# A fixed order for the opening of an attention-plus-expert-layer kernel: engine queues in the order of the text, block means by small transfers, weights staged in whole chunks

## The chip, the cores and the metric

The kernel runs on one core of a Trainium2 chip. The core has five engines that work side by side: TensorE (matrix products, PE in the profile), VectorE (DVE), ScalarE (ACT), GpSimd (POOL) and SyncE (SP), which here only issues transfers. Each engine takes its instructions strictly in the order of its own queue and waits on semaphores for the others; transfers run on sixteen DMA engines. The metric is the time of one execution on the device in microseconds. A change in the median of under 0.5% is not told from none here.

## What is computed

The reference is local attention with block summaries, followed by a two-layer expert with a rational activation. Batch 4, 8 heads, 768 positions, head size 64; the 3072 tokens of width 512 then go through 512 to 2048 to 512.

```python
k_sum = k.reshape(B, H, nb, 32, D).max(axis=3)
v_sum = v.reshape(B, H, nb, 32, D).mean(axis=3)
scores_l = where(|pos_q - pos_k| < 16, scale * q @ k.T, -1e9)
scores_s = scale * q @ k_sum.T + log(32)
a = softmax(concat([scores_l, scores_s]))      # with 1e-9 added to the sum
x = a @ concat([v, v_sum])                     # then heads side by side: 3072 x 512
h = x @ w_in
P = a0 + a1*h + a2*h^2 + a3*h^3
Q = 1 + |b0|*|h| + |b1|*h^2
out = (P / (Q + 1e-6)) @ w_out
```

The weights arrive as 64-bit floats and are turned into 32-bit values on the chip.

## The kernel before

**Tiles.** Attention works on 48 pieces ("halves") of 64 query positions. One half has four pairs of heads; each query sees 96 keys of its window and 24 block maxima (120 columns). Three functions carry a half: `att_a` (scores on TensorE into `sc`, mask and minimum on VectorE, exponentials on ScalarE, the reciprocal on VectorE, the scaling by it on GpSimd: tile `ss`), `att_b` (four transposes into `pt` on TensorE, a copy to `pts` on ScalarE) and `att_c` (products with values into `av`, stored as a rounded high part `xh` and a remainder `xl`). Eight halves make a group of 512 tokens.

**The expert.** There are six groups (g = 0 to 5) and 16 chunks of the hidden width (fc = 0 to 15), so 96 steps. A step multiplies into `h` (`moe1`, twelve matmuls: high by high, low weights by high, high by low), evaluates the activation (`gelu`: six ScalarE operations with a logarithm and an exponential, five or six on VectorE, and one on GpSimd that makes the low part `gl`), and three steps later (LAG) multiplies the result of the earlier chunk into four accumulators `po` (`moe2`). Halves of the next group's attention are spread over the steps.

**Weights.** A chunk is loaded as 64-bit words (1 MB for both matrices) into a staging tile `wr`, and `w_split` converts it: ScalarE rescales the upper words (L295), VectorE shifts the lower words (L298) and joins them in (L299), ScalarE rounds to the high part (L302), GpSimd makes the low part (L304). Chunks 0 to 7 end in `wearly`, the others in `w` tiles. Before, chunks 0 to 7 are staged whole in four buffers `wl`. Chunks 8 to 15 are staged as two halves of 512 KB in the pool `stage`, which has two buffers and also holds rows for the key maxima `kr` and value sums `vr`. Converted weights stay in SBUF for all groups.

**The opening.** The first eight halves are computed before step 0. Their block means of values come from TensorE (`vf`, L153, raw values times a matrix of 1/32), and are copied by ScalarE into rows 96 to 119 of six value tiles (L158 to L160); halves 6 and 7 reuse the tiles of halves 0 and 1.

**Order.** The text is traced and a scheduler with its own timeline reorders instructions of each engine between their dependencies; `tc.high_priority` shifts its priorities. In the 96 steps the matmuls are kept in the order of the text (`chained`); before step 0 no engine is. The string FIRST gives the order of the first loads on SP's queue.

Of the kernel before, what the change touches and what calls it, by code (L numbers as in the profile page):

```python
# [10 lines left out]
I32 = mybir.dt.int32  # L11
# [3 lines left out]
PSUM = bass.MemoryType.PSUM  # L15

# [25 lines left out]
CVL = 5  # L42
NEARLY = 3
SOFF = 12
VLAG = 5
NWARM = 6
FIRST = "Q0 K0 K1 V0 K2 K3 Q1 V1 S V2 W0 V3 F W1 V4 W2 G W3 V5"
AVGAT = 4
# [10 lines left out]
def tile_kernel(ctx, tc, qw_in, kraw, kwin, vpad, vred, wio, a, b, cmask, cident, cavg, out):  # L59
# [6 lines left out]
    wl = ctx.enter_context(tc.tile_pool(name="wl", bufs=NLATE))  # L66
# [7 lines left out]
    chained = []  # L74

    def mm(*args, **kw):
        ins = nc.tensor.matmul(*args, **kw)  # L77
        if chained:
            tc.keep_in_program_order(ins)
# [20 lines left out]
    def setup():  # L100
# [4 lines left out]
        nc.vector.tensor_scalar_mul(cs[:, 0:6], coef, SH)  # L105
        nc.vector.tensor_scalar_mul(cs[:, 6:7], cs[:, 5:6], -1.0)
        nc.vector.tensor_tensor(cs[:, 5:6], cs[:, 5:6], cs[:, 6:7], op=ALU.max)
        nc.vector.memset(cs[:, 7:8], C1 * SH)
# [16 lines left out]
    def key_sum(bi, pr):  # L125
        kr = sums.pop(("k", bi, pr))
        ins = nc.vector.tensor_reduce(ksum[bi][:, pr, :], kr.rearrange("p (n k) -> p n k", k=BLK), axis=AX.X, op=ALU.max)
        if bi:
            tc.keep_in_program_order(ins)
# [8 lines left out]
    def value_sum(bi, c):  # L138
        vs, vr = vsum[bi], sums.pop(("v", bi, c))
        tc.keep_in_program_order(nc.vector.tensor_reduce(vs[:, c, :], vr, axis=AX.X, op=ALU.add))  # L140
        if c == NVC - 1:
            nc.vector.tensor_scalar_mul(vs, vs, 1.0 / BLK)
# [9 lines left out]
    def value_average(bi, av, vt, i):  # L152
        nc.tensor.matmul(av[:NK, :], avg[:, AVGW - NK - 4 * i:AVGW - 4 * i], vt[i], start=(i == 0), stop=(i == len(vt) - 1))  # L153
        if i < len(vt) - 1:
            return
        if bi == 0:
            for i in range(2):
                nc.scalar.copy(vw[i][NKW:NK, :], av[NKW:NK, :])  # L158
            for t in vres[2:6]:
                nc.scalar.copy(t[NKW:NK, :], av[NKW:NK, :])  # L160
        else:
            t = gp.tile([NK, DM], F32, tag="gh", name="vn")
            nc.scalar.copy(t[NKW:NK, :], av[NKW:NK, :])
# [10 lines left out]
    def att_a(jj, pool=None, tag="a", sbuf=None):  # L174
        bi, j = divmod(jj, NJ)
        kt, qt = kw[jj % 2], qw[jj % 2] if jj >= HPG else qres[:, jj]
        if j < 2 and bi > 0 or jj in (HPG, HPG + 1):
            nc.vector.tensor_copy(kt[:, NKC - 1], ksum[bi])
        mt = mask[:, 0 if j == 0 else (2 if j == NJ - 1 else 1), :]
        sc = (pool or ps_a).tile([P, 512], F32, tag=tag, name=f"sc{jj}")  # L180
        for pr in range(NPAIR):
# [4 lines left out]
            for lo, hi, keys in parts:  # L186
                for e in range(2):
                    rows = slice(e * D, (e + 1) * D)
                    mm(sc[rows, pr * NK + lo:pr * NK + hi], qt[rows, pr, :], keys[rows], start=True, stop=True)
# [3 lines left out]
        for pr in range(NPAIR):  # L193
            nc.vector.tensor_tensor_reduce(  # L194
                out=ss[:, pr, :], in0=sc[:, pr * NK:(pr + 1) * NK], in1=mt, op0=ALU.add, op1=ALU.min,
                scale=-SCALE, scalar=3.0e38, accum_out=sm[:, 0, pr:pr + 1])
        for pr in range(NPAIR):
# [320 lines left out]
```

## Time and profile before

| what | value |
|---|---|
| median of three runs | 726.27 us (725.87 to 729.55) |
| profiled execution | 721.27 us |
| its span, first to last instruction | 719.5 us |
| busy share of the span: TensorE, VectorE, ScalarE, GpSimd | 94%, 84%, 66%, 44% |
| moved by DMA | 60.8 MB, 84 GB/s on the mean |

A line number such as L298 is a line of the kernel; where a helper records all matmuls (L77), one tells them by tile names. "out<-in" names the tile written and the tiles read, x16 a count. The span is cut into the opening, group 0 (16 steps) and the rest. Idle time of an engine counts only where the end waits for it.

### The profile page before, as it was taken

What the parts mean: (1) busy time and instruction counts of PE and PEld (TensorE: products, weight loads), DVE (VectorE), ACT (ScalarE), POOL (GpSimd) and SP (SyncE); (2) the same over time, 40 slices, a digit from 0 to 9 for tenths busy, and PEclk for the clock granted to TensorE, in tenths of its full rate; (3) what the DMA queues carried; (4) which work ended last, traced back from release to release, by engine and by line L of the source; (5) the groups of instructions that cost most, each with busy time, mean ns of one, the idle gap of its engine ahead of it and who ended that gap; (6) DMA issues with size and microseconds to landing.
All of it is one profiled execution on the core that took longest, in us unless ns stands there. A gap on an engine that the chain in (4) does not pass through costs nothing.

```text
span 719.5 us, 12003 instructions
## 1 busy us (share of the span) xinstructions
PE 677.4 (94%) x4196; PEld 526.5 (73%) x4196; DVE 604.6 (84%) x1189; ACT 471.5 (66%) x1058; POOL 313.7 (44%) x328
## 2 busy tenths in 40 slices
PE   8887879948999999999999999999999999999997
PEld 5555657736777777777777777777777777888886
DVE  4688997797988898887789998878978878998885
ACT  2896776656776666776666766656776755775562
POOL 0785645645554354444343345443453353232231
PEclk9887989978999999999999999999999999999999
DMA  9982254333124231113112332111121200010001
GB/s 288 368 279 89 85 167 139 118 98 118 40 76 149 87 91 32 44 62 119 47 43 74 103 95 69 48 45 30 51 82 45 60 12 0 1 59 1 1 1 59
DMA packets 30681, 60.76 MB, mean 84 GB/s; under 512 B 3748, under 2 KB 15396, under 8 KB 29596
## 3 DMA queue, kind: packets, MB, share of 16 engines
q1 hardware_dynamic: 29916, 59.54, 26.0%
q8 instruction: 33, 0.54, 0.3%
q10 hardware_dynamic: 576, 0.25, 0.1%
q14 instruction: 28, 0.23, 0.1%
q0 software_dynamic: 128, 0.20, 0.1%
HBM read 53.44 MB, written 6.34 MB: 83 GB/s over the span
## 4 chain that ended last, share of the span: by engine, by line
PE 70%; DVE 9%; ACT 7%; DMA 6%; POOL 4%; issue 4%; SPq 0%; DVEq 0%; POOLq 0%; ACTq 0%
PE po L77 31%; PE h L77 29%; PE sc L77 4%; DMA wr<-in_wio_dram 4%; PE av L77 3%; PE pt L221 3%; ACT ss L198 2%; POOL ss L203 2%; DVE tq L326 2%; POOL w L304 1%; DVE wr L299 1%; ACT wr L295 1%; PE vf L153 1%; DVE gh L331 1%; DMA kres<-in_kraw_dram 1%
## 5 line engine op out<-in xcount | busy, mean ns | idle before, releaser
L334 POOL TENSOR_TENSOR gl<-tu,ta 128x512 fp32r<-128x512 f32 x96 | 132.8, 1383 | 219.5 <-DVE tu L333 143.5
L203 POOL TENSOR_SCALAR ss<-ss,sm 128x120 f32<-128x120 f32 x192 | 132.5, 707 | 142.1 <-ACT ta L328 105.3
L326 DVE SCALAR_TENSOR_TENSOR tq<-tq,cs,ta 128x512 f32<-128x512 f32 x96 | 117.4, 1223 | 41.9 <-ACT ta L324 41.1
L323 ACT ACTIVATE tq<-h 128x512 f32<-128x512 f32 x96 | 57.2, 596 | 121.5 <-PE h L77 121.5
L77 PE MATMUL po<-w,gh 128*128 128x512 f32 x384 | 130.6, 422 | 0.0
L77 PE MATMUL po<-wearly,gh 128*128 128x512 f32 x384 | 130.1, 420 | 0.0
L327 ACT ACTIVATE ta<-tq,cs 128x512 f32<-128x512 f32 x96 | 69.6, 725 | 60.6 <-DVE tq L326 60.2
L77 PE MATMUL h<-xh,wearly 128*128 128x512 f32 x384 | 98.2, 399 | 1.5 <-ACT xh L251 1.1
L77 PE MATMUL h<-xh,w 128*128 128x512 f32 x384 | 95.4, 390 | 0.0
L331 DVE SCALAR_TENSOR_TENSOR gh<-tu,cs,ta 128x512 fp32r<-128x512 f32 x96 | 73.4, 765 | 22.3 <-ACT ta L328 14.4
L77 PEld LDWEIGHTS h<-xh,wearly 128*128 128x128 f32 x384 | 73.7, 193 | 17.8 <-ACT xh L251 1.3
L77 PEld LDWEIGHTS h<-xh,w 128*128 128x128 f32 x384 | 72.2, 188 | 15.9
L198 ACT ACTIVATE ss<-ss,sm 128x120 f32<-128x120 f32 x192 | 73.0, 383 | 11.0 <-DVE sm L194 10.9
L77 PEld LDWEIGHTS po<-w,gh 128*128 128x128 f32 x384 | 67.5, 195 | 16.4 <-issue 3.5
L77 PEld LDWEIGHTS po<-wearly,gh 128*128 128x128 f32 x384 | 65.5, 192 | 16.8 <-issue 3.4
L333 DVE SCALAR_TENSOR_TENSOR tu<-tu,cs,tq 128x512 f32<-128x512 f32 x96 | 75.1, 782 | 3.1
L77 PE MATMUL po<-w,gl 128*128 128x512 f32 x192 | 76.7, 400 | 0.0
L77 PE MATMUL po<-wearly,gl 128*128 128x512 f32 x192 | 75.9, 395 | 0.0
L221 PE MATMUL pt<-ident,ss 128*120 128x128 f32 x192 | 53.6, 291 | 23.6 <-POOL ss L203 23.3
L325 ACT ACTIVATE tu<-h,cs 128x512 f32<-128x512 f32 x96 | 75.0, 782 | 0.0
L330 DVE SCALAR_TENSOR_TENSOR tu<-tu,cs,h 128x512 f32<-128x512 f32 x96 | 71.6, 746 | 2.9
L332 DVE SCALAR_TENSOR_TENSOR tq<-tq,gh 128x512 f32<-128x512 f32 x96 | 67.6, 704 | 2.8
(63 smaller groups left out, 1043.3 us busy)
## 6 DMA issues: line engine op xcount, KB each, us to landing
vw<-in_vpad_dram SPq DMA_DIRECT2D x44, 192.0 KB, 2.7
wr<-in_wio_dram SPq DMA_DIRECT2D x8, 1024.0 KB, 10.9
wr<-in_wio_dram SPq DMA_DIRECT2D x16, 512.0 KB, 3.9
kw<-in_kwin_dram SPq DMA_DIRECT2D x40, 192.0 KB, 2.7
out_dram<-o SPq DMA_DIRECT2D x24, 256.0 KB, 2.1
qw<-in_qw_dram SPq DMA_DIRECT2D x40, 128.0 KB, 2.6
kr<-in_kraw_dram SPq DMA_DIRECT2D x12, 384.0 KB, 3.3
vr<-in_vred_dram SPq DMA_DIRECT2D x8, 384.0 KB, 3.5
```

The source lines that it names most:

```text
L77: ins = nc.tensor.matmul(*args, **kw)
L198: nc.scalar.activation(ss[:, pr, :], ss[:, pr, :], AF.Exp, scale=-1.0, bias=sm[:, 0, pr:pr + 1], accum_out=sm[:, 1, pr:pr + 1])
L203: nc.gpsimd.tensor_scalar(ss[:, pr, :], ss[:, pr, :], sm[:, 1, pr:pr + 1], 1.0, op0=ALU.mult, op1=ALU.mult)
L221: ins = nc.tensor.transpose(out=pt[:NK, pr * P:(pr + 1) * P], in_=ss[:, pr, :], identity=ident)
L325: nc.scalar.activation(tu, h, AF.Identity, scale=cs[:, 3:4], bias=cs[:, 2:3])
L326: nc.vector.scalar_tensor_tensor(out=tq, in0=tq, scalar=cs[:, 5:6], in1=ta, op0=ALU.mult, op1=ALU.add)
L327: nc.scalar.activation(ta, tq, AF.Ln, bias=cs[:, 7:8])
L330: nc.vector.scalar_tensor_tensor(out=tu, in0=tu, scalar=cs[:, 1:2], in1=h, op0=ALU.add, op1=ALU.mult)
L331: nc.vector.scalar_tensor_tensor(out=gh, in0=tu, scalar=cs[:, 0:1], in1=ta, op0=ALU.add, op1=ALU.mult)
L332: nc.vector.scalar_tensor_tensor(out=tq, in0=tq, scalar=C1 * SH, in1=gh, op0=ALU.add, op1=ALU.mult)
L333: nc.vector.scalar_tensor_tensor(out=tu, in0=tu, scalar=cs[:, 0:1], in1=tq, op0=ALU.add, op1=ALU.subtract)
L334: nc.gpsimd.tensor_tensor(gl, tu, ta, op=ALU.mult)
```

## The change

1. **A wrapper `Kept` around four engines.** While an engine is in `strict`, each of its instructions is tied behind the one recorded before it, so its queue has the order of the text. All four are strict from the first score product to the end of the string EARLY. Then VectorE, ScalarE and GpSimd are released, but everything they do later stays tied behind their last strict instruction. TensorE stays strict to the end.
2. **EARLY** writes the order of the opening: `s` scores and minima, `e` exponentials and scaling, `p`/`P` transposes (with `P` the copy to `pts` is on VectorE), `v` a product of the means, `w` and `x` the two parts of converting chunk 0, `c` products with values, `W` a whole conversion. Chunks 1 and 2 come after the last `c`.
3. **Means by transfers.** ScalarE copies them to two value tiles; six others get them by a transfer of 24 rows each from the first, on SP's queue. Halves 6 and 7 have value tiles of their own.
4. **Weights staged whole.** All chunks but 15 are loaded as 1 MB into four separately named buffers; the load of a later chunk is issued when an earlier one is rounded. VectorE's two operations take both matrices at once (1024 columns in place of twice 512).
5. CVL goes from 5 to 3 (a conversion is recorded three steps ahead of its use), two attention loads move ahead of the opening's computation, and the means of batch 1 move from before step 0 into steps 0 and 1.

```diff
-CVL = 5
+CVL = 3
-FIRST = "Q0 K0 K1 V0 K2 K3 Q1 V1 S V2 W0 V3 F W1 V4 W2 G W3 V5"
+FIRST = "K0 Q0 K1 K2 K3 S Q1 F W0 V0 V1 V2 V3 V4 V5 V6 V7 W1 A8 A9 W2 G W3"
+EARLY = ("s0 s1 e0 s2 e1 s3 e2 v0 s4 e3 P0 v1 s5 e4 P1 v2 s6 e5 P2 v3 s7 w0 e6 P3 v4 e7 P4 x0 v5 c0 P5 c1 P6 c2 "
+         "P7 c3 c4 c5 c6 c7 W1 W2")
...
+    class Kept:
...
+                out = getattr(self.engine, name)(*args, **kw)
+                for ins in nc.cur_bb.bb.instructions[n:]:
+                    if ins.engine == out.ins.engine:
+                        if self.last is not None:
+                            tc.add_manual_dep(ins, self.last, ORDERED, reason="order of the text")
+                        if self in strict:
+                            self.last = ins.name
...
             for i in range(2):
-                nc.scalar.copy(vw[i][NKW:NK, :], av[NKW:NK, :])
-            for t in vres[2:6]:
-                nc.scalar.copy(t[NKW:NK, :], av[NKW:NK, :])
+                act.copy(vw[i][NKW:NK, :], av[NKW:NK, :])
+            for t in vres[2:]:
+                nc.sync.dma_start(out=t[NKW:NK, :], in_=vw[0][NKW:NK, :])
...
     def w_load(fc):
+        kind = F32 if wio.dtype == F32 else I32
+        words = DM if kind == F32 else 2 * DM
+        if fc == NFC - 1:
+            raws[fc] = [(slice(s, s + 1), stage.tile([P, 1, words], kind, tag="st", name=f"wr{fc}_{s}")) for s in range(2)]
+        else:
+            k = fc % NLATE if fc < NFC - NLATE else fc - (NFC - NLATE) + 1
+            raws[fc] = [(slice(0, 2), wl.tile([P, 2, words], kind, tag=f"wl{k}", name=f"wr{fc}"))]
+        for s, raw in raws[fc]:
+            nc.sync.dma_start(out=raw, in_=wio[fc, :, s, :].bitcast(kind))
+
+    def w_join(fc):
...
+            act.activation(top, top, AF.Prelu, scale=2.0**-112, alpha=2.0**32)
+            dve.tensor_single_scalar(l32, l32, 29, op=ALU.logical_shift_right)
+            dve.scalar_tensor_tensor(out=h32, in0=h32, scalar=3, in1=l32,
+                                     op0=ALU.logical_shift_left, op1=ALU.bitwise_or)
+
+    def w_round(fc):
...
+            act.copy(wt[:, 0, s, :], w)
+            for i in range(s.start, s.stop):
+                gps.tensor_tensor(wt[:, 1, i, :], w[:, i - s.start], wt[:, 0, i, :], op=ALU.subtract)
+        ahead = fc + NLATE if fc < NFC - 2 * NLATE else fc + NLATE - 1
+        if fc != NFC - 2 * NLATE and ahead < NFC:
+            w_load(ahead)
...
+    strict |= {pe, dve, act, gps}
+    for what in EARLY.split():
...
+    strict -= {dve, act, gps}
...
-        at(max(fc - CVL, 0), lambda fc: w_split(fc, wr.pop(fc) if fc in wr else w_load(fc)), fc)
+        at(max(fc - CVL, 0), w_split, fc)
...
+        if step in (0, 1):
+            if step == 0:
+                vf = ps_o.tile([P, DM], F32, tag="o", name="vf1")
+            for i in range(3 * step, 3 * step + 3):
+                value_average(1, vf, fv1, i)
```

The next excerpts show the built order of a queue. The first number in a name is the program's own: `wr5` is the staging tile of chunk 5 (`wr8_1` its second half), `av6` belongs to half 6, `gl0_2` to group 0, chunk 2. In the changed kernel every operation through the wrapper has the line L87.

VectorE at the end of the opening, before:

```order
L298 TENSOR_SCALAR wr5_0_676<-wr5_0_676 128x512 x2
L252 TENSOR_TENSOR xl0_412<-av2_517,xh0_411 128x4x64
L299 SCALAR_TENSOR_TENSOR wr5_0_676<-wr5_0_676 128x512 x2
L252 TENSOR_TENSOR xl0_412<-av3_535,xh0_411 128x4x64
L252 TENSOR_TENSOR xl0_412<-av4_546,xh0_411 128x4x64
L298 TENSOR_SCALAR wr6_0_749<-wr6_0_749 128x512 x2
L299 SCALAR_TENSOR_TENSOR wr6_0_749<-wr6_0_749 128x512 x2
L252 TENSOR_TENSOR xl0_412<-av5_557,xh0_411 128x4x64
L252 TENSOR_TENSOR xl0_412<-av6_568,xh0_411 128x4x64
L298 TENSOR_SCALAR wr7_0_828<-wr7_0_828 128x512 x2
L299 SCALAR_TENSOR_TENSOR wr7_0_828<-wr7_0_828 128x512 x2
L252 TENSOR_TENSOR xl0_412<-av7_579,xh0_411 128x4x64
```

VectorE at the same place, after the change:

```order
L87 TENSOR_TENSOR xl0_495<-av3_550,xh0_494 128x4x64
L87 TENSOR_TENSOR xl0_495<-av4_561,xh0_494 128x4x64
L87 TENSOR_TENSOR xl0_495<-av5_572,xh0_494 128x4x64
L87 TENSOR_TENSOR xl0_495<-av6_583,xh0_494 128x4x64
L87 TENSOR_TENSOR xl0_495<-av7_594,xh0_494 128x4x64
L87 TENSOR_SCALAR wr1_158<-wr1_158 128x1024
L87 SCALAR_TENSOR_TENSOR wr1_158<-wr1_158 128x1024
L87 TENSOR_SCALAR wr2_164<-wr2_164 128x1024
L87 SCALAR_TENSOR_TENSOR wr2_164<-wr2_164 128x1024
```

The conversions of chunks 1 to 7, which stood among and before the remainders `xl`, now stand behind the last of them.

GpSimd in the first steps, before:

```order
L304 TENSOR_TENSOR wearly_103<-wr7_0_828,wearly_103 128x512 x2
L334 TENSOR_TENSOR gl0_0_645<-tu0_0_643,ta0_0_641 128x512
L203 TENSOR_SCALAR ss8_729<-ss8_729,sm8_730 128x120 x4
L334 TENSOR_TENSOR gl0_1_706<-tu0_1_704,ta0_1_702 128x512
L203 TENSOR_SCALAR ss9_801<-ss9_801,sm9_802 128x120 x4
L334 TENSOR_TENSOR gl0_2_778<-tu0_2_776,ta0_2_774 128x512
L304 TENSOR_TENSOR w8_905<-wr8_0_906,w8_905 128x512
L334 TENSOR_TENSOR gl0_3_857<-tu0_3_855,ta0_3_853 128x512
L203 TENSOR_SCALAR ss10_971<-ss10_971,sm10_972 128x120 x4
L304 TENSOR_TENSOR w8_905<-wr8_1_908,w8_905 128x512
L334 TENSOR_TENSOR gl0_4_939<-tu0_4_937,ta0_4_935 128x512
```

GpSimd at the same place, after the change:

```order
L87 TENSOR_TENSOR wearly_103<-wr6_619,wearly_103 128x512 x2
L87 TENSOR_TENSOR gl0_0_638<-tu0_0_636,ta0_0_634 128x512
L87 TENSOR_TENSOR gl0_1_683<-tu0_1_681,ta0_1_679 128x512
L87 TENSOR_SCALAR ss9_782<-ss9_782,sm9_783 128x120 x4
L87 TENSOR_TENSOR wearly_103<-wr7_657,wearly_103 128x512 x2
L87 TENSOR_TENSOR w8_1063<-wr8_732,w8_1063 128x512 x2
L87 TENSOR_TENSOR w8_1063<-wr9_815,w8_1063 128x512 x2
L87 TENSOR_TENSOR w10_1219<-wr10_890,w10_1219 128x512 x2
L87 TENSOR_TENSOR gl0_2_759<-tu0_2_757,ta0_2_755 128x512
L87 TENSOR_TENSOR w10_1219<-wr11_981,w10_1219 128x512 x2
L87 TENSOR_SCALAR ss10_943<-ss10_943,sm10_944 128x120 x4
L87 TENSOR_TENSOR gl0_3_836<-tu0_3_834,ta0_3_832 128x512
```

Before, one half chunk stands between two activations' low parts; now the low part of chunk 2 stands behind four whole chunks of weights.

SP's queue where the means are copied (a row `x2` is two transfers), after the change only, since there were no such transfers:

```order
L303 DMA wr2_164<-in_wio_dram 128x2048
L166 DMA vf1_0_166<-in_vpad_dram 128x4x512
L166 DMA vf1_1_168<-in_vpad_dram 128x2x512
L303 DMA wr3_170<-in_wio_dram 128x2048
L178 DMA vr0_110<-vw0_100 24x512
L178 DMA vr1_111<-vw0_100 24x512
L178 DMA vr2_112<-vw0_100 24x512
L178 DMA vr3_113<-vw0_100 24x512
L178 DMA vlast_114<-vw0_100 24x512 x2
L235 DMA vw0_100<-in_vpad_dram 96x512
L303 DMA wr4_483<-in_wio_dram 128x2048
```

The six copies stand behind the loads of chunks 2 and 3 and of batch 1's raw values, and ahead of chunk 4's.

More of the change, by code (lines that the diff above doesn't have):

```diff
@@ L188, in att_a @@
                     rows = slice(e * D, (e + 1) * D)
-                    mm(sc[rows, pr * NK + lo:pr * NK + hi], qt[rows, pr, :], keys[rows], start=True, stop=True)
+                    pe.matmul(sc[rows, pr * NK + lo:pr * NK + hi], qt[rows, pr, :], keys[rows], start=True, stop=True)
         sbuf, stag = sbuf or (pp, "p")
@@ new lines, in w_round @@
+        wt = weights(fc)
+        for s, raw in raws.pop(fc):
+            w = raw if wio.dtype == F32 else raw.rearrange("p i (n t) -> p i n t", t=2)[:, :, :, 1].bitcast(F32)
+            act.copy(wt[:, 0, s, :], w)
[4 more added lines that the diff above has]
+            w_load(ahead)
```

205 lines of the change are left out of this document (97 added, 108 removed).

## The prediction

> **What bounds the kernel now.** I read the windows first, cut at two points: the first matmul of the first expert layer chunk (step 0 of group 0) and the first of group 1. The columns are the busy time of TensorE, weight loads, VectorE, ScalarE and GpSimd, then granted clock, DMA share and GB/s.
>
> ```profile
> 0.00:59.42 59.42, 45.80 (x453) 28.78 (x453) 41.97 (x128) 39.92 (x103) 34.98 (x50) 0.85 0.89 301
> 59.42:192.49 133.07, 111.29 (x656) 84.76 (x657) 112.98 (x227) 90.38 (x204) 72.39 (x71) 0.89 0.34 106
> 192.49:719.50 527.01, 520.31 (x3089) 413.00 (x3087) 449.68 (x836) 341.17 (x752) 206.31 (x210) 1.00 0.18 55
> ```
>
> After 192.49 us TensorE is busy for 520.31 of 527.01 us at full clock: it is the bound, and the order of every engine there is the same in both kernels but for buffer numbers. So I carry 527.0 us over unchanged, and the question is when group 1 begins. Ahead of it stand a prologue of 59.4 us (attention of the first 512 tokens) and group 0, 133.1 us. The timeline of TensorE (start, duration, instruction, idle time before it and who ended it) and, below it, the chain of waits give the cuts, the first matmul of step 9 and the steady rate:
>
> ```profile
> 57.20 1.12 PE L77 MATMUL av<-pts,vw 120*64 120x64 f32 x16 [4.31 <-DVE xl L252]
> 59.42 3.47 PE L77 MATMUL h<-xh,wearly 128*128 128x512 f32 x8 [1.09 <-ACT xh L251]
> ...
> 127.04 2.00 PE L77 MATMUL h<-xh,w 128*128 128x512 f32 x8
> ...
> 192.49 1.99 PE L77 MATMUL h<-xh,wearly 128*128 128x512 f32 x8
> ...
> 245.77 2.75 PE h L77 x12
> ...
> 259.03 2.75 PE h L77 x12
> ```
>
> Two steps take 259.03 - 245.77 = 13.26 us, so sixteen at TensorE's pace would take 106 us at most. Group 0 takes 133.1, so something else bounds it. VectorE is busy there for 112.98 us (85%) and idle for 20.1. The chain of waits inside group 0, and the waits, say what makes it idle:
>
> ```profile
> 79.44 4.01 DMA wr<-in_wio_dram
> ...
> 89.90 4.76 DMA kr<-in_kraw_dram
> ...
> 95.67 4.32 DMA wr<-in_wio_dram
> ...
> 129.91 5.16 DMA wr<-in_wio_dram
> ...
> 161.32 4.21 DMA wr<-in_wio_dram
> ...
> ACT wr L295 <- DMA wr<-in_wio_dram: 13.1, 9, 2.6
> ...
> DVE wr L298 <- DMA wr<-in_wio_dram: 9.0, 10, 2.0
> ...
> DVE tq L326 <- ACT ta L324: 4.7, 4, 2.7
> ...
> DVE gh L331 <- ACT ta L328: 3.3, 2, 3.0
> ```
>
> The half chunks of late weights pass through two staging buffers, so a load starts only when a conversion has ended, and its 4 to 5 us lie on the chain. VectorE waits 9.0 us for such loads itself, and ScalarE 13.1 with the layer's logarithms queued behind.
>
> **The change, part by part.** *Start of group 0.* In the new order matmuls of the first output (av2 to av7) need the block means by six transfers on SP, which stand behind all loads up to chunk 3.
>
> ```profile
> 0.00:20.00 20.00, 14.68 (x158) 9.19 (x158) 10.03 (x43) 6.47 (x23) 2.43 (x9) 1.00 0.92 295
> 20.00:40.00 20.00, 19.35 (x179) 12.08 (x180) 13.67 (x48) 17.47 (x46) 14.79 (x22) 0.83 1.04 370
> ...
> wr<-in_wio_dram SPq DMA_DIRECT2D x7, 1024.0 KB, 11.8
> ...
> vw<-in_vpad_dram SPq DMA_DIRECT2D x4, 192.0 KB, 8.6
> ...
> vw<-in_vpad_dram SPq DMA_DIRECT2D x44, 192.0 KB, 2.7
> ...
> out_dram<-o SPq DMA_DIRECT2D x24, 256.0 KB, 2.1
> ```
>
> (The first four rows are of the first 40 and 45 us, the last two of the whole run.) Ahead of the copies the program loads keys 1.64 MB, queries 1.05, constants 0.32, four weight chunks 4.19, values 1.57, two tiles of raw values 3.15 and two attention inputs 0.66: 12.6 MB. The first 20 us moved 5.9 MB at 295 GB/s; the other 6.7 at 370 take 18.1 us; so this traffic ends at 38 us, the 0.3 MB of copies at 39, seen as landed 2.1 later: 41 us. Six outputs follow, each of an av, an xh and an xl of these rows (the first row is ScalarE's copy of the means, the third its copy of a transposed score tile):
>
> ```profile
> 31.49 1.07 ACT L158 COPY vw<-vf 24x512 f32<-24x512 f32 x2 [0.42 <-PE vf L153]
> ...
> 33.64 0.69 PE L77 MATMUL av<-pts,vw 120*64 120x64 f32 x16
> ...
> L227 ACT COPY pts<-pt 120x512 f32<-120x512 f32 x8 | 4.5, 580 | 0.5 <-PE pt L221 0.5
> ...
> L251 ACT CAST xh<-av 128x256 fp32r<-128x256 f32 x8 | 2.9, 374 | 0.0
> ...
> L252 DVE TENSOR_TENSOR xl<-av,xh 128x256 fp32r<-128x256 f32 x7 | 2.7, 411 | 0.0
> ```
>
> That is 0.69 + 0.37 + 0.41 = 1.5 us for one, two overlapping in two PSUM buffers, with signals about 1.0 each: **group 0 starts at 47 us, 12.4 earlier.** If the copies didn't queue, they would be landed 2.7 us after ScalarE's copies, which now end at 31.49 + 1.07 = 32.6, and group 0 would start at 41; if all 12.9 MB went at the prologue's 301 GB/s, at 51. I take 47, since loads issued in the first 45 us landed after 8.6 to 11.8 us, not 2.7. The Trainium skill, DMA: Bandwidth & Descriptors, Anatomy of one DMA, gives about 2.0 us fixed cost and little for 48 KB, by which a copy would be landed near 35 us and the sum be 6 us lower; the 8.6 us above, for 192 KB in the same stretch, speak against it here.
>
> The eight score copies that move from ScalarE to VectorE, 0.58 us each there, are 4.6 us. VectorE's prologue work becomes 42.0 - 25.5 (conversions, below) + 2.7 (chunk 0) + 4.6 = 24 of 47 us, so its idle time covers them; without it they cost their 4.6. ScalarE loses four mean copies of 0.5 us, which is worth nothing where the outputs wait for transfers.
>
> *VectorE in group 0.* So far seven conversions besides chunk 0 stood in the prologue's gaps; now chunks 1 to 15 all stand behind the last xl. The first two rows are the windows again, for the conversions' tiles alone (VectorE, ScalarE, GpSimd); the others give least, median and greatest nanoseconds of each operation:
>
> ```profile
> 0.00:59.42 59.42, 25.54 (x30) 16.94 (x15) 19.34 (x14) 0.85 0.89 301
> 59.42:192.49 133.07, 25.48 (x35) 22.18 (x33) 27.82 (x20) 0.89 0.34 106
> ...
> L298 DVE TENSOR_SCALAR wr<-wr x32: 400/432/1533, 17.9 to 178.4; 128x512 int32<-128x512 int32 x32
> L299 DVE SCALAR_TENSOR_TENSOR wr<-wr x32: 661/686/1798, 19.1 to 179.4; 128x512 int32<-128x512 int32 x32
> L304 POOL TENSOR_TENSOR w<-wr,w x16: 1301/1326/1777, 86.7 to 180.9; 128x512 fp32r<-128x512 f32 x16
> ```
>
> VectorE's first column: 51.0 us for 32 halves, 1.59 a half, of which 1.12 is the two medians and 0.47 waiting beside GpSimd. A whole chunk now is one pair of operations: 2 x 1.12 + 0.47 = 2.7 us. Its bounds are the minima without waiting, 2.1, and twice the present mean, 3.2. Fifteen cost 40.7 (32 to 48), in place of 25.5: VectorE's work in group 0 becomes 113.0 + 15.2 = **128.2 us** (119 to 136).
>
> *Its idle time.* Four staging buffers of a whole chunk take the loads off the chain: minus the 9.0 us, and half of the 8.0 us behind ScalarE, leaves 7 of 20.1. What is late next is GpSimd's product of layer chunk 2, which now stands behind those of weights 7 to 10. So TensorE's steps 3 to 8 wait more than before. Afterwards no conversion is left: steps 9 to 15, which took 65.4 us (127.04 to 192.49), can go at 6.6 us a step, 46 in all. The sum holds both, since it counts VectorE's work. TensorE's granted clock, 0.89 in group 0, I leave as it is: its waits before step 9 stay, and VectorE, not TensorE, sets that stretch. Moving the later split from five to three steps ahead I cost at nothing: the scheduler has placed them early all the same. The second batch's averages, now in steps 0 and 1, cover waits for VectorE there.
>
> *Sum.* 47 + 128.2 + 7 = 182.2 us for the start of group 1, **10.3 before 192.5**. The profiled execution took 721.27 us (span 719.5 plus 1.8), so it would take 711.0. The median of the runs shown, 726.27, is 5.0 above that execution; from it, **716**.
>
> **The rivals.** *The port decides (slower).* The conversions and their GpSimd products now stand packed together. An operation of 400 ns took up to 1533, one of 661 up to 1798: up to 1.13 us of waiting, near one GpSimd product of 1.30. If the 30 operations wait 0.8 us each instead of 0.23, group 0 grows by 17 us and the time becomes 733; from 0.57 us a wait the gain is gone. For it: GpSimd has 30 products of at least 1.30 us in the same stretch, 39 us. Against: of the longer operations there are half as many to be caught. The Trainium skill, SBUF — State Buffer, Who interferes with whom, says that a VectorE operation in two-port mode and one of GpSimd exclude each other, the second blocking for the whole of the first; the maxima above agree with it.
>
> *In-order waits replace the loads (same or slower).* ScalarE's queue now has conversions ahead of the layer's logarithms. If VectorE stays 85% busy as now, 128.2 / 0.85 = 151 us end at 198, 5 later: 732. It breaks even at 128.2 / (192.5 - 47) = 88%. With 86 to 90% the time is within 0.5% of before.
>
> *A larger gain.* With the copies early (43) and VectorE's work at 124 with 4 us idle, group 1 starts at 171: 705. Against it stands the queue above.
>
> *The means copies hold the start back.* At 51 us the forecast loses 4: 720. This shifts the likeliest case, without turning it.
>
> **How the numbers follow.** The likeliest case (with the late start) gets 0.51, the larger gain 0.12, no measurable change 0.12, the port 0.13, the in-order waits 0.12 beyond that. Faster by over 0.5% (the measurement's limit, 3.6 us) 0.63, the same 0.12, slower 0.25. The likeliest one's own range is 707 to 722; 704 to 731 leaves about a tenth on either side.
>
> **What would show it.** Group 0's first matmul near 47 us, after a VectorE and TensorE gap of several us that mean copies end; waits for weight loads near zero after that; VectorE over 93% busy until the last conversion; the first matmul of group 1 near 182, and 527 us behind it. A conversion that takes over 3.4 us (two operations of 1.7), or VectorE under 88% busy from the start of group 0 to its end, would make the forecast wrong.

## The result, and the profile after

The changed kernel takes 729.9 us (median of 20 runs, 724.69 to 732.9), the kernel before 723.85 (20 runs, 718.89 to 729.55). The ratio is 1.0079, with a 95% interval of 1.0056 to 1.0102: slower by 0.8%, where 716 was forecast from 726.27, faster by 1.4%. The profiled execution takes 731.92 us, its span 730.1.

The windows of the changed kernel, with the columns as in the prediction (length, then TensorE, weight loads, VectorE, ScalarE, GpSimd, granted clock, DMA share, GB/s). The cuts are the first matmul of group 0, of its step 9, and of group 1; the fourth row is the whole of group 0:

```profile
0.00:49.24 49.24, 37.00 (x441) 25.72 (x441) 23.63 (x107) 20.41 (x78) 13.82 (x38) 0.86 0.90 292
49.24:152.82 103.58, 68.88 (x373) 50.37 (x373) 94.17 (x152) 73.16 (x135) 76.14 (x59) 0.84 0.45 155
152.82:199.56 46.74, 46.71 (x297) 36.72 (x296) 36.08 (x74) 30.40 (x71) 20.08 (x23) 1.00 0.13 39
49.24:199.56 150.32, 115.59 (x668) 87.09 (x669) 130.25 (x226) 103.56 (x204) 96.22 (x81) 0.89 0.35 119
199.56:730.10 530.54, 521.88 (x3089) 414.35 (x3087) 451.40 (x836) 341.26 (x752) 208.16 (x210) 1.00 0.18 54
```

Group 0 starts 10.2 us earlier (49.24 for 59.42), but takes 150.3 us in place of 133.1, so group 1 starts 7.1 us later. VectorE's work in group 0 is close to the forecast (130.25 for 128.2). Its idle time is not: 150.32 - 130.25 = 20.1 us, as much as before, where 7 had been expected. About half of it, 103.58 - 94.17 = 9.4, lies in steps 0 to 8, and 46.74 - 36.08 = 10.7 in steps 9 to 15, where TensorE never waits and VectorE has too little to do.

TensorE's timeline at the start of group 0 shows the means (a transfer ends the wait, at 42.31):

```profile
42.31 1.12 PE L87 MATMUL av<-pts,vr 120*64 120x64 f32 x16 [6.60 <-DMA vr<-vw]
...
49.24 2.14 PE L87 MATMUL h<-xh,wearly 128*128 128x512 f32 x8 [0.47 <-ACT xh L87]
```

The waits in steps 0 to 8 (49.24 to 152.82 us; engine, tile and line, what released it, total, count, longest), above them one row of the kernel before, for the whole of its group 0:

```profile
PE pt L221 <- POOL ss L203: 17.7, 8, 9.1
...
PE pt L87 <- POOL ss L87: 24.3, 4, 9.4
...
PE h L87 <- ACT ta L87: 8.5, 1, 8.5
...
DVE wr L87 <- DMA wr<-in_wio_dram: 3.6, 1, 3.6
ACT wr L87 <- DMA wr<-in_wio_dram: 3.0, 1, 3.0
```

The waits for weight loads did go: 6.6 us in place of 9.0 + 13.1. TensorE waits 24.3 us, in four pieces, for scaled scores from GpSimd, 6.6 more than in group 0 before, and once 8.5 us for the tile of `h`, which is new. The profile puts this wait down to ScalarE's exponential, which ends at 69.76 us; but by the kernel's text that operation doesn't read `h`, and VectorE's second product with `h` ends at 69.73, so what TensorE waited for isn't settled. The conversions themselves, by the windows for their tiles (VectorE, ScalarE, GpSimd):

```profile
0.00:49.24 49.24, 1.92 (x2) 2.41 (x3) 2.56 (x2) 0.86 0.90 292
49.24:199.56 150.32, 36.92 (x32) 34.43 (x32) 48.50 (x30) 0.89 0.35 119
```

VectorE spends 1.92 us on them in the opening, where it spent 25.54 before, and 36.92 in group 0, where it spent 25.48.

### The profile page after: what moved, and what is told of

Same layout as the page of the kernel before. It is cut to its first block, busy times and chain, and to the rows that moved or that the text cites. A ratio compares the mean times of both kernels' runs of the same rounds, so it can differ in the third digit from the quotient of the medians.

```text
span 730.1 us, 11932 instructions
## 1 busy us (share of the span) xinstructions
PE 674.5 (92%) x4196; PEld 527.2 (72%) x4196; DVE 605.3 (83%) x1167; ACT 465.2 (64%) x1032; POOL 318.2 (44%) x328
## 4 chain that ended last, share of the span: by engine, by line
PE 74%; POOL 7%; DVE 6%; issue 5%; DMA 4%; ACT 3%; SPq 0%; POOLq 0%; DVEq 0%; ACTq 0%
PE po L87 33%; PE h L87 30%; PE sc L87 5%; POOL ss L87 3%; PE av L87 3%; PE pt L87 2%; DMA wr<-in_wio_dram 2%; POOL wearly L87 2%; DVE tq L87 2%; POOL w L87 1%; DMA kres<-in_kraw_dram 1%; ACT ta L87 1%; DVE tu L87 1%; DVE gh L87 1%; ACT ss L87 1%
## 5 line engine op out<-in xcount | busy, mean ns | idle before, releaser
L87 POOL TENSOR_TENSOR gl<-tu,ta 128x512 fp32r<-128x512 f32 x96 | 134.7, 1403 | 227.7 <-DVE tu L87 158.9
L87 POOL TENSOR_SCALAR ss<-ss,sm 128x120 f32<-128x120 f32 x192 | 131.0, 700 | 136.1 <-ACT ta L87 104.6
L87 DVE SCALAR_TENSOR_TENSOR tq<-tq,cs,ta 128x512 f32<-128x512 f32 x96 | 117.3, 1222 | 45.4 <-ACT ta L87 44.7
L87 ACT ACTIVATE tq<-h 128x512 f32<-128x512 f32 x96 | 57.3, 597 | 138.1 <-PE h L87 129.6
L87 PE MATMUL po<-wearly,gh 128*128 128x512 f32 x384 | 134.6, 433 | 0.0
L87 PE MATMUL po<-w,gh 128*128 128x512 f32 x384 | 128.7, 417 | 0.0
L87 PE MATMUL h<-xh,wearly 128*128 128x512 f32 x384 | 97.8, 397 | 9.3 <-ACT ta L87 8.5
L87 ACT ACTIVATE ta<-tq,cs 128x512 f32<-128x512 f32 x96 | 69.8, 727 | 56.7 <-DVE tq L87 56.1
L87 DVE SCALAR_TENSOR_TENSOR gh<-tu,cs,ta 128x512 fp32r<-128x512 f32 x96 | 75.7, 788 | 24.7 <-ACT ta L87 17.6
L87 PE MATMUL h<-xh,w 128*128 128x512 f32 x384 | 95.3, 390 | 0.0
L87 PEld LDWEIGHTS h<-xh,wearly 128*128 128x128 f32 x384 | 73.1, 191 | 26.9 <-ACT ta L87 9.3
L87 PEld LDWEIGHTS h<-xh,w 128*128 128x128 f32 x384 | 72.1, 188 | 15.7
L87 ACT ACTIVATE ss<-ss,sm 128x120 f32<-128x120 f32 x192 | 73.1, 383 | 15.4 <-DVE sm L87 15.3
L87 PEld LDWEIGHTS po<-wearly,gh 128*128 128x128 f32 x384 | 67.5, 198 | 18.6 <-issue 4.9
L87 PE MATMUL pt<-ident,ss 128*120 128x128 f32 x192 | 52.5, 298 | 29.0 <-POOL ss L87 28.5
L87 PEld LDWEIGHTS po<-w,gh 128*128 128x128 f32 x384 | 66.2, 191 | 16.9 <-issue 3.1
L87 PE MATMUL po<-wearly,gl 128*128 128x512 f32 x192 | 77.8, 405 | 0.0
L87 DVE SCALAR_TENSOR_TENSOR tu<-tu,cs,tq 128x512 f32<-128x512 f32 x96 | 74.3, 774 | 3.0
L87 PE MATMUL po<-w,gl 128*128 128x512 f32 x192 | 75.9, 395 | 0.0
L87 ACT ACTIVATE tu<-h,cs 128x512 f32<-128x512 f32 x96 | 75.1, 782 | 0.0
L87 DVE SCALAR_TENSOR_TENSOR tu<-tu,cs,h 128x512 f32<-128x512 f32 x96 | 71.7, 746 | 3.0
L87 DVE SCALAR_TENSOR_TENSOR tq<-tq,gh 128x512 f32<-128x512 f32 x96 | 69.1, 719 | 3.0
```

What stands on the lines that cost most here:

```text
L87: out = getattr(self.engine, name)(*args, **kw)
```

## The experiments

Three theories stood at the start. The **pile**: the conversions of chunks 3 to 10 stand ahead of the activations of steps 0 to 6, so TensorE waits early and VectorE late. The **port**: VectorE and GpSimd hold each other up more than before. The **loads**: a staging buffer comes free only behind GpSimd's product, so weight loads still set the pace. A fourth, the **idle opening**, came from the first four runs. The table collects what the windows of each profiled execution say (us; idle is a window's length less VectorE's busy time in it), with the ratio of the medians to those of the kernel before on the same chip (it took 725.1 us beside the first four experiments, 725.85 beside the next four, 723.1 beside the last):

| kernel | VectorE's work, opening and group 0 | its idle time in the opening | in group 0 | group 1 starts | median | ratio (95%) |
|---|---|---|---|---|---|---|
| before | 155.0 | 17.5 | 20.1 | 192.5 | 723.85 | 1 |
| changed | 153.9 | 25.6 | 20.1 | 199.6 | 729.9 | 1.0079 (1.0056 to 1.0102) |
| means by ScalarE | 155.4 | 18.1 | 18.6 | 192.1 | 725.46 | 1.0002 (0.9982 to 1.0023) |
| spread | 157.9 | 24.9 | 11.1 | 193.9 | 726.64 | 1.0003 (0.9981 to 1.0024) |
| before, whole staging alone | 150.2 | 24.4 | 12.3 | 186.9 | 720.74 | 0.9928 (0.9902 to 0.9955) |
| changed, old staging | 151.6 | 23.9 | 19.3 | 194.8 | 729.59 | 1.0050 (1.0028 to 1.0073) |
| no tie | 151.9 | 25.4 | 17.0 | 194.3 | 727.89 | 1.0026 (1.0002 to 1.0050) |
| chunks 1, 2 in the opening | 152.4 | 20.2 | 18.2 | 190.7 | 724.12 | 0.9986 (0.9963 to 1.0010) |
| the same, means by ScalarE | 156.4 | 15.1 | 17.6 | 189.1 | 721.15 | 0.9957 (0.9931 to 0.9984) |
| the same, spread by four | 152.1 | 15.8 | 15.7 | 183.5 | 719.50 | 0.9920 (0.9891 to 0.9949) |
| the same, sums earlier | 151.3 | 16.8 | 15.1 | 183.2 | 711.84 | 0.9846 (0.9781 to 0.9912) |
| the same, spread by five | 153.7 | 18.1 | 9.6 | 181.4 | 710.32 | 0.9818 (0.9741 to 0.9895) |

In a row of the table, work and the two idle times add up to group 1's start. Between before and changed that sum grows by 7.1 us: the work falls by 1.1, the idle time in group 0 stays the same, and the idle time in the opening grows by 8.2. Idle time in the opening is no loss by itself: with whole staging alone it is 24.4 us, since VectorE has less work there (35.3 us for 42.0), and group 1 starts earlier. It is one where work that could stand in it comes later instead.

**Means copied by ScalarE.**

```diff
             for t in vres[2:]:
-                nc.sync.dma_start(out=t[NKW:NK, :], in_=vw[0][NKW:NK, :])
+                act.copy(t[NKW:NK, :], av[NKW:NK, :])
```

> The changed kernel, but ScalarE copies the block means to the other six value tiles; the six small transfers are gone. If the transfers hold the start back, as forecast, the first matmul of group 0 moves from 49.2 us to 41 to 43. Then two outcomes: if group 0 is a queue of work that moves along with its start, the time falls by the same 6 to 8 us, to 722 to 724 beside 730; if the weight loads freed by GpSimd set the pace of group 0, its end stays at 199 to 200 us and the time at 729 to 731.

```profile
0.00:41.89 41.89, 34.76 (x440) 23.47 (x440) 23.76 (x107) 22.98 (x84) 13.77 (x38) 0.92 0.98 334
41.89:192.10 150.21, 115.56 (x668) 86.97 (x669) 131.59 (x226) 103.16 (x204) 96.06 (x81) 0.85 0.35 120
```

Group 0 starts at 41.9 us. The transfers hold it back by 7.4. Group 0 then takes 150.2 us, as it did: it moves along as a whole, which speaks against the loads. The time falls by 0.8%, some 4 to 6 us, a little less than group 1's start and than was written down (725.5 for 722 to 724). So the kernel without the transfers is level with the kernel before (1.0002), but not faster.

**Conversions spread.**

```diff
+TIE = 4
...
+            first = act.activation(top, top, AF.Prelu, scale=2.0**-112, alpha=2.0**32)
+            second = dve.tensor_single_scalar(l32, l32, 29, op=ALU.logical_shift_right)
+            if fc - TIE in acted:
+                for ins, name in zip((first, second), acted[fc - TIE]):
+                    tc.add_manual_dep(ins.ins, name, ORDERED, reason="behind an activation")
```

> The changed kernel, with the two first operations of the conversion of chunk fc (ScalarE's rescaling, VectorE's shift) each tied behind the activation of chunk fc - 4 on the same engine; nothing else is altered. Theory of the pile (conversions of chunks 3 to 10 stand ahead of the activations of steps 0 to 6, so TensorE idles early and VectorE late): VectorE's work stays near 130 us, its idle time falls from 20 us to 7 or less, TensorE's idle time in steps 0 to 8 falls from 35 us to under 20; group 0 takes 130 to 137 us in place of 150, the time is 711 to 717. Theory of the port (VectorE and GpSimd hold each other up): the same operations meet the same products, group 0 takes 145 us or more, 725 or more. Theory of the loads (a staging buffer comes free only behind GpSimd's product): no load starts earlier, group 0 takes 148 or more, 728 or more.

Group 0, its steps 9 to 15, and the conversions' tiles up to 200 us (in the last row VectorE stands first):

```profile
48.58:193.86 145.28, 116.42 (x669) 86.95 (x669) 134.23 (x224) 102.35 (x204) 98.51 (x81) 0.92 0.36 123
...
132.84:193.86 61.02, 50.31 (x298) 38.23 (x296) 54.04 (x88) 40.49 (x82) 42.65 (x34) 0.94 0.20 64
...
0.00:200.00 200.00, 43.38 (x34) 35.97 (x34) 49.70 (x32) 0.91 0.49 163
```

About a third of what the pile theory expected. VectorE's idle time does fall by 9 us, to 11.1, and it is 92% busy. But its work grows by 4.0: the conversions cost 43.4 us where they cost 38.8 packed together. TensorE's idle time in steps 0 to 8 falls from 34.7 to 18.2 us, as expected, but steps 9 to 15, where the late conversions now stand, take 61.0 us in place of 46.7. Group 0 takes 145.3 us and the time is 726.6, which is what was written down for the port; the runs with fills, below, go against that reading. So the spread order is worth some 5 us in group 1's start, and the pile isn't the whole of the loss.

**Whole staging alone, in the kernel before.** All of part 4 of the change, with no other part:

```diff
-    wl = ctx.enter_context(tc.tile_pool(name="wl", bufs=NLATE))
+    wl = ctx.enter_context(tc.tile_pool(name="wl", bufs=1))
...
-        w_split(fc, wr.pop(fc) if fc in wr else w_load(fc))
+        w_split(fc)
```

> The kernel before, with the whole staging alone (part 4 of the change); no fixed order, no transfers of means. Theory of the pile: whole staging lets the scheduler place four to five conversions in a row, so group 0 grows from 133 us to 140 to 150, and the time from 724 to 730 to 740, by this part alone. Theory of the loads, as forecast: the loads leave the chain, group 0 loses up to 13 us, the time is 711 to 718. If the pile comes from the tie behind the opening instead, this kernel is within 3 us of before.

Opening, steps 0 to 8 and steps 9 to 15, and VectorE's wait for weights in group 0:

```profile
0.00:59.67 59.67, 48.51 (x452) 31.13 (x452) 35.28 (x114) 39.84 (x103) 31.80 (x49) 0.84 0.89 312
59.67:140.22 80.55, 60.54 (x361) 46.06 (x362) 77.47 (x133) 57.56 (x118) 59.01 (x48) 0.86 0.42 143
140.22:186.88 46.66, 46.66 (x298) 36.71 (x296) 37.45 (x79) 31.41 (x72) 21.43 (x23) 1.00 0.14 39
...
DVE wr L289 <- DMA wr<-in_wio_dram: 0.7, 1, 0.7
```

Faster than before, by 0.7%. The forecast's mechanism is right for this part by itself: VectorE's wait for loads falls from 9.0 to 0.7 us, its idle time in group 0 from 20.1 to 12.3. The time, 720.7, stays above the 711 to 718 written down for it, as group 0 loses 5.9 us and not 13. Whole staging alone doesn't bring the loss that the pile theory had put down to it: here too steps 9 to 15 run at TensorE's pace (46.66 us) and VectorE idles 9.2 us in them, but only nine conversions are left for group 0, and steps 0 to 8 take 80.6 us, not 103.6.

**The changed kernel with the old staging.**

```diff
-        for s, raw in raws[fc]:
-            nc.sync.dma_start(out=raw, in_=wio[fc, :, s, :].bitcast(kind))
...
+        for s in [slice(0, 2)] if fc < NSTG else [slice(0, 1), slice(1, 2)]:
...
+            pool, tag = (wl, "wl") if n == 2 else (stage, "st")
```

> The changed kernel with the old staging (chunks 8 to 15 as halves through two buffers); order, ties and transfers of means as changed. Theory of the pile with whole staging as its cause: the small buffers spread the conversions by themselves, group 0 takes 131 to 138 us and the time is 711 to 718. Pile by the tie behind the opening: group 0 takes 145 to 152 as now, 725 to 732. Theory of the loads as in the forecast (half chunks on the chain cost about 13 us more): group 0 takes 155 or more, 735 or more.

```profile
47.77:194.76 146.99, 115.83 (x669) 85.39 (x669) 127.66 (x254) 104.65 (x218) 91.45 (x80) 0.90 0.38 122
...
ACT wr L87 <- DMA wr<-in_wio_dram: 17.0, 12, 3.9
...
DVE wr L87 <- DMA wr<-in_wio_dram: 12.6, 9, 3.7
```

With the old staging VectorE's operations take 512 columns again. The waits for loads are all back, 29.6 us where whole staging has 6.6. Yet VectorE's idle time is 19.3, group 1 even starts 4.8 us earlier than in the changed kernel, and the time is that kernel's within the intervals. In this order the loads weren't what made VectorE idle; other waits take their place. The outcome is the one written down for the tie behind the opening.

**No tie behind the opening.**

```diff
     strict -= {dve, act, gps}
+    dve.last = act.last = gps.last = None
```

> The changed kernel, but what comes after the opening is no longer tied behind the opening's last instruction on VectorE, ScalarE and GpSimd; the order inside the opening stays. Theory of the idle opening (VectorE has nothing to do for 25.6 of the opening's 49.2 us, because the tie keeps the conversions of chunks 1 to 15 out of it): three or four conversions of 2.5 us move into the opening's waits, group 0 starts at 48 to 51 us and group 1 at 188 to 193 in place of 199.6, the time is 718 to 724. Rival, late weights (chunks 1 to 3 land too late to fill the opening): nothing moves by more than 2 us, 728 to 732.

```profile
0.00:51.72 51.72, 37.66 (x440) 26.70 (x441) 26.33 (x112) 23.70 (x81) 16.41 (x40) 0.80 0.88 298
51.72:194.33 142.61, 115.69 (x669) 86.06 (x670) 125.59 (x221) 100.24 (x201) 96.14 (x79) 0.90 0.35 118
```

A miss for both. The scheduler moved only a little of VectorE's work into the opening (26.3 us in place of 23.6), which starts group 0 2.5 us later and leaves 25.4 us idle. Group 1 is 5.2 us earlier all the same, and the time lies between the two forecasts. To lift the tie doesn't fill the opening.

**Chunks 1 and 2 written into the opening.** Only the string changes:

```diff
-... c0 P5 c1 P6 c2 P7 c3 c4 c5 c6 c7 W1 W2
+... c0 P5 c1 P6 W1 W2 c2 P7 c3 c4 c5 c6 c7
```

> The changed kernel, with the conversions of chunks 1 and 2 written into the wait for the transfers of the means (between the transposes of half 6 and the products of half 2) instead of behind the opening. Theory of the idle opening: group 0 starts at 49 to 50 us as now, VectorE's work in group 0 falls by 5 us, group 1 starts at 193 to 196 and the time is 723 to 727. Theory of the loads (chunk 4 and later, freed one by one, set the end of group 0): the end stays at 198 to 200 us, the time at 728 to 732.

```profile
0.00:48.21 48.21, 34.98 (x440) 23.98 (x441) 28.04 (x111) 24.42 (x82) 19.96 (x42) 0.89 0.95 320
48.21:190.70 142.49, 114.12 (x669) 85.38 (x669) 124.31 (x222) 98.69 (x200) 91.94 (x77) 0.89 0.34 118
```

VectorE does 4.4 us more in the opening, which isn't longer for it, and 5.9 less in group 0; group 1 starts 8.9 us earlier, at 190.7 where 193 to 196 was written down: 1.0 is the start, 5.9 the work and 1.9 less idle time. The time, 724.1, is where the idle opening puts it. The end of group 0 followed, so the loads don't set it.

**Both, with a copy of the means one half ahead.**

```diff
-            for t in vres[2:]:
-                nc.sync.dma_start(out=t[NKW:NK, :], in_=vw[0][NKW:NK, :])
...
+            if 1 < n + 1 < HPG:
+                act.copy(vres[n + 1][NKW:NK, :], vw[0][NKW:NK, :])
             att_c(n)
...
+... c0 P5 c1 w1 P6 c2 P7 x1 c3 c4 w2 c5 c6 c7 x2
```

> The changed kernel without the small transfers: ScalarE copies the means into two value tiles, and from there into each other tile one half ahead of its use; the conversions of chunks 1 and 2 stand between the products of halves 1 to 7 instead of behind them. Theory of the idle opening: the gains of the two single edits add, group 0 starts at 42 to 44 us, VectorE's work in it is 5 us less than 131.6, group 1 starts at 187 to 190, the time is 718 to 722. Rival: the conversions push the products back by as much as they take, group 0 starts at 47 or later and the time is 724 or more.

```profile
0.00:43.23 43.23, 33.09 (x440) 22.48 (x441) 28.18 (x111) 27.21 (x87) 16.44 (x40) 0.95 0.99 333
43.23:189.12 145.89, 117.52 (x669) 88.66 (x669) 128.26 (x222) 100.17 (x201) 95.03 (x79) 0.85 0.35 121
```

The start, group 1 and the time are all in the ranges of the idle opening; VectorE's work in group 0 falls by 3.3 us, not 5. VectorE's idle time in the opening is down from 25.6 to 15.1 us, and group 1 starts 10.4 us earlier than in the changed kernel. But the gains of the two single edits don't add, as had been expected: they were 7.5 and 8.9 us, 16.4 together. Presumably a part was counted twice: each edit makes use of the wait for the transfers, the one by removing it and the other by filling it.

**The same, spread by four.** The edit is that of the spread run.

> The kernel of the run before (means copied by ScalarE, chunks 1 and 2 converted in the opening) with the conversions spread, each tied behind the activation of the chunk four before. If the pile and the idle opening are separate losses, another 4 to 5 us go: 713 to 718. If VectorE's work is by now the whole length of group 0 (idle time there under 12 us already), spreading brings nothing more: 718 to 722.

```profile
43.89:183.54 139.65, 115.72 (x668) 87.45 (x669) 123.98 (x221) 99.97 (x201) 90.10 (x79) 0.88 0.37 127
183.54:713.90 530.36, 522.00 (x3089) 414.28 (x3087) 450.67 (x837) 341.64 (x752) 207.81 (x210) 1.00 0.18 54
```

Group 1 starts another 5.6 us earlier, as much as spreading brought alone. The medians differ by less than their intervals, so by time alone the two expectations aren't told apart; the condition of the second, idle time under 12 us, wasn't met (17.6). The ten times lie between 716.4 and 722.7 us, and the profiled execution is the fastest of them. This time most of it came as less work for VectorE (124.0 for 128.3), in the first spread run as less idle time with more work; how the gain divides is not settled by one profile of each.

**GpSimd's products replaced by fills**, in the changed kernel and in the kernel before:

```diff
-                gps.tensor_tensor(wt[:, 1, i, :], w[:, i - s.start], wt[:, 0, i, :], op=ALU.subtract)
+                gps.memset(wt[:, 1, i, :].bitcast(F32), 0.0)
```

> The changed kernel, with GpSimd's 32 products for the low parts of the weights replaced by fills with zero (so the low parts of the weights are missing from the result); a fill reads nothing, waits for no conversion and is short. Theory of the port (VectorE is held up beside GpSimd's products): VectorE's work in the opening and group 0, 153.9 us, falls by 10 us or more, to 144 or less, with the conversions at 2.0 us a chunk in place of 2.4. Theory of the pile alone: VectorE's work stays within 4 us, and only its idle time changes. In both, staging buffers come free earlier and GpSimd's queue is short, so group 0 should end 10 to 20 us earlier.

> The kernel before with the same replacement (low parts of the weights missing). Port: VectorE's work in the opening and group 0, 155.0 us, falls by 12 to 16 us, since the 64 operations of its 32 half conversions lose their 0.47 us of waiting a half, to 139 to 143. Without a port effect it stays at 151 to 155. Set beside the run on the changed kernel this tells whether the change made VectorE wait more for GpSimd (its fall is larger there) or less.

Changed kernel with fills, opening and group 0:

```profile
0.00:51.06 51.06, 35.93 (x440) 24.23 (x440) 23.69 (x107) 20.06 (x78) 20.69 (x56) 0.83 0.86 282
51.06:179.62 128.56, 111.32 (x668) 84.47 (x669) 111.84 (x226) 101.94 (x204) 53.52 (x63) 0.93 0.41 139
```

Its conversions' tiles in group 0 (VectorE first):

```profile
51.06:179.62 128.56, 30.18 (x32) 34.25 (x32) 0.93 0.41 139
```

Kernel before with fills, opening and group 0, and its conversions' tiles in group 0:

```profile
0.00:55.62 55.62, 44.26 (x452) 27.69 (x453) 32.75 (x129) 39.52 (x103) 24.73 (x58) 0.89 0.93 322
55.62:177.25 121.63, 107.07 (x656) 82.10 (x657) 103.68 (x226) 89.74 (x204) 50.63 (x61) 0.94 0.38 116
...
55.62:177.25 121.63, 22.85 (x34) 22.16 (x33) 0.94 0.38 116
```

VectorE's work falls from 153.9 to 135.5 us in the one, and from 155.0 to 136.4 in the other: 18.4 and 18.5 us, in the second more than the 12 to 16 written down. So VectorE is held up beside these products, by 0.6 us for each of the 32, but by as much before the change as after: VectorE's side of the port isn't the cause. GpSimd's side isn't excluded, as its 32 products take 51.1 us in the changed kernel and 47.2 before. Of the 7.1 us by which the change puts off group 1, 2.4 are left with fills (179.6 against 177.3; 708.75 us against 705.36, one run each). So GpSimd's products seem to take part in the loss, most likely through their place in the queues, since scores and staging buffers wait for them. The fills also let the scheduler order group 0 otherwise, so these 4.7 us aren't divided further.

**Later batches' sums four steps earlier, and the conversions a step earlier.**

```diff
-SOFF = 12
+SOFF = 16
...
-TIE = 4
+TIE = 5
```

The first pair of lines is in both runs, the second in the second run alone.

> The fastest kernel so far (means copied by ScalarE, chunks 1 and 2 converted in the opening, conversions spread), with the loads and sums of the later batches 16 steps ahead of their use in place of 12, so that no value sum stands beside step 49. If step 49 is long (11.1 us in place of 7.4) because VectorE's sums hold GpSimd's scaling back, it falls to 7.5 or less and the time goes 3 to 4 us below 719.5, to 715 to 717. If the cause is another, step 49 stays above 10 us and the time at 718 to 721.

> The same with each conversion tied behind the activation five chunks before it, not four, so that conversions run a step earlier. Pile: one step earlier brings part of the pile back, TensorE waits 2 to 4 us more in steps 1 to 8, 2 to 4 us slower than with four. If conversions come too late with four (TensorE's waits in steps 8 and 11, 7.1 and 9.6 us, are for late products), it is 3 to 6 us faster.

With the sums earlier, step 49 and everything behind group 0:

```profile
405.21:411.22 6.01, 6.01 (x29) 4.61 (x28) 4.98 (x9) 2.63 (x7) 4.33 (x6) 1.00 0.04 15
183.18:709.60 526.42, 520.33 (x3089) 412.84 (x3087) 450.25 (x837) 341.17 (x752) 206.07 (x210) 1.00 0.18 53
```

With the tie at five as well, group 0 and behind it:

```profile
45.05:181.38 136.33, 115.48 (x669) 87.14 (x670) 126.78 (x220) 99.20 (x201) 94.93 (x79) 0.92 0.39 131
181.38:707.60 526.22, 520.35 (x3089) 412.88 (x3087) 450.21 (x838) 341.31 (x752) 205.75 (x209) 1.00 0.17 53
```

Step 49 takes 6.0 us in place of 11.1, and the rest 526.4 in place of 530.4: 4.0 us go, as expected if the sums are the cause (the edit moves the batches' loads as well). The median fell by more (7.7), of which 2.8 is this chip, where the kernel before took 723.1 in place of 725.85; so the time, 711.8, is also below the 715 to 717 written down. With the tie at five VectorE is idle for 9.6 us in group 0, 5.5 less, and group 1 is 1.8 earlier, but the medians, 711.84 and 710.32, aren't told apart, and neither expectation is met. The last kernel is 1.8% faster than the kernel before, with the changed kernel's wrapper and staging, and its order but for chunks 1 and 2.

## Why the prediction was wrong, point by point

- **The start at 47 us: right in its mechanism, 2.2 short.** A transfer of the means ends the wait, at 42.3 where 41 was worked out, and the six outputs behind it take 6.9 us where 6 had been allowed; so group 0 starts at 49.24, inside 41 to 51. Without the transfers it starts at 41.9, near the lower bound, which had been worked out for transfers that don't queue. The 2.0 us that the prediction quotes from the Trainium skill stand in that section for transfers issued by GpSimd; these are issued by SP, from 31.8 to 36.7 us, and the wait ended 5.6 us after the last.
- **VectorE's work, 128.2: right in its sum (130.25), by two errors that cancel.** The fifteen conversions cost 36.9 us, not 40.7: taken whole they cost 2.5 us each. VectorE's other work in group 0 costs 130.25 - 36.92 = 93.3, not 112.98 - 25.48 = 87.5. With fills 30.18 us of conversions and 111.84 - 30.18 = 81.7 of the rest are left, so the others are held up beside GpSimd for 11.7 us; by the same subtraction it was 87.5 - (103.68 - 22.85) = 6.7 before the change. The conversions lost 5.5 us of waiting (12.2 with the opening before, 6.7 after), and the other operations took over about as much.
- **"Four staging buffers of a whole chunk take the loads off the chain": right, but not worth its price here.** Waits for loads fell from 22.1 to 6.6 us in the changed kernel, and VectorE's idle time from 20.1 to 12.3 where whole staging was put into the kernel before. In the changed order the same idle time came back from other engines' results.
- **"Leaves 7 of 20.1", and "the sum holds both, since it counts VectorE's work": this step failed.** Idle time was 20.1 us, 13.1 more than forecast, out of 17.4 us by which group 1's start was missed (199.6 for 182.2; the start gives 2.2, VectorE's work 2.1). The prediction had both halves of it in hand: TensorE's steps 3 to 8 would wait more, and steps 9 to 15 would go at TensorE's pace, 46 us in all (46.7 measured). But if TensorE sets the pace of steps 9 to 15, VectorE's work there, 36.1 us, doesn't fill them, and those 10.7 us are to be added to the sum, not hidden in it. Summed by stage, with the measured 36.1 taken off the 128.2, 92.1 us of work and 7 idle in steps 0 to 8 and then 46 behind a start at 47 give 192 for group 1, and 726 us: no gain. What is left of the miss is spread over the start, the work and the waits of steps 0 to 8.
- **The opening, "its idle time covers them".** It covered the moved score copies: VectorE's work there is 23.6 us, where 24 was worked out. That the kernel before kept seven conversions besides chunk 0 in this idle time is in the prediction's sum too, as 15.2 us more work in group 0; so this step didn't fail. But it leaves 23 us of the opening idle (25.6 measured), and the whole gain then hung on the idle time of group 0. The runs that fill it again (chunks 1 and 2 earlier: 8.9 us; with the means by ScalarE: 10.4) take back what the change had lost.
- **The rest, 527.0 carried over: 530.5 measured.** Nearly all of the difference is step 49 (below), which the change doesn't touch; the profiled execution of before was spared. It was the exception: of the ten profiled kernels with GpSimd's products and the sums in their old place, the other nine take 530.2 to 531.6, the kernel before with whole staging among them (530.7). How often each kernel meets it was not measured.
- **The rivals.** The in-order waits came true in number: VectorE is 130.25 / 150.32 = 87% busy against the break-even of 88%, and that rival's price was 732. The prediction had named a share under 88% as what would make it wrong. Its mechanism, logarithms behind conversions on ScalarE, isn't shown: the one wait of 8.5 us that could be it may as well be VectorE's, and the other increase in TensorE's waits, 6.6 us, is for scores from GpSimd. The port is refuted as a cause on VectorE's side. The Trainium skill, SBUF — State Buffer, Who interferes with whom, says that a VectorE instruction with two SBUF inputs contends with a GpSimd instruction that reads SBUF, not with one that only writes it. The runs with fills, which only write, agree (18 us less work), but the effect is the same on both sides of the change.
- **The later split, five steps ahead to three, costed at nothing**, was not tried by itself.

## What to carry to other kernels

A sum over a stretch with two bounds has to be made stage by stage: where one engine sets the pace, the other's idle time there is part of the length, however much work it has elsewhere. An opening that gets shorter gains only if the work that stood in its gaps has another gap to go to; so count the bounding engine's idle time from the very start, before and after, and fill the opening's waits by hand when an order is fixed by hand. Spread work that competes with a pipeline over its steps, which was worth 5 to 6 us in the start of group 1 here, with VectorE's work growing in one of two runs.

## What had not been expected of the hardware

A short wait at one step can cost about twice itself. In step 49 of the two kernels the four scalings on GpSimd (ss) wait equally long for VectorE, and then take 2.60 us in one execution and 3.69 in the other. Kernel before, GpSimd and TensorE:

```profile
417.28 2.60 POOL L203 TENSOR_SCALAR ss<-ss,sm 128x120 f32<-128x120 f32 x4 [2.96 <-DVE sm L201]
...
418.03 0.32 PE L221 MATMUL pt<-ident,ss 128*120 128x128 f32 x1 [1.28 <-POOL ss L203]
```

Changed kernel, GpSimd and TensorE, and then a window of TensorE's clock (0.50, the third number from the end of its row):

```profile
424.80 3.69 POOL L87 TENSOR_SCALAR ss<-ss,sm 128x120 f32<-128x120 f32 x4 [2.96 <-DVE sm L87]
...
425.56 0.32 PE L87 MATMUL pt<-ident,ss 128*120 128x128 f32 x1 [1.91 <-POOL ss L87]
...
427.86 0.32 PE L87 MATMUL pt<-ident,ss 128*120 128x128 f32 x1 [1.28 <-POOL ss L87]
...
428.35:431.76 3.41, 3.41 (x11) 2.50 (x10) 0.68 (x1) 0.79 (x2) 1.40 (x2) 0.50 0.01 2
```

TensorE waits 1.28 us in the one and 1.91 + 1.28 in the other, and in the second the granted clock falls to half for the next 3.41 us: the step takes 11.1 us in place of 7.5. The longer waits make up 1.9 of these 3.7 us, and half the stretch at half clock, 1.7 (an estimate from the two figures), nearly all the rest. Why the scalings took 1.1 us longer with the same order of work around them isn't settled. Nor is it settled when a wait brings the fall: in the nine profiles whose rest takes 530.2 us or more, step 49 has a wait of 1.91 to 2.23 us and half clock behind it, but in the run spread by five, waits of 3.07 and 2.00 us in group 0 (they end at 74.40 and 164.86 us) are followed by full clock. Moving VectorE's sums out of that step removes the wait and the drop, and is worth 4.0 us of the span.
